# Fewer, wider products of zeros at the start, and one block's loads in another order, in a fused state-space scan and ELU feed-forward kernel

## The chip, the cores and the metric

The kernel runs on one core of a Trainium2 chip. The metric is the device time of one execution in microseconds; 338.59 us is the median of three runs before the change. The engines are TensorE (PE in the profile, PEld for its weight loads), VectorE (DVE), ScalarE (ACT), GpSimd (POOL) and SyncE (SP), whose queue issues nearly all DMAs.

## The reference

Two stages, one after the other. The first is a state-space scan over `x` (4 batches, 8 heads, 768 tokens, 32 features) with decays `a` and vectors `B`, `C` of length 16, in chunks of 32 tokens:

```
cum = cumsum(log(clip(a)))                    # within a chunk
y   = (C B^T * exp(cum_i - cum_j), causal) x  # inside the chunk
    + C state * exp(cum)                      # from earlier chunks
state = exp(sum) * state + sum_j B_j x_j exp(cum_end - cum_j)
```

The second takes the 3072 x 256 result as `x` and computes `elu(x @ w_in) @ w_out`, with `w_in` 256 x 2048 and `w_out` 2048 x 256. The weights arrive as 64-bit floats.

## The kernel before, in words

Tokens are worked in 12 blocks of 256, numbered n from 0; a pair of blocks shares buffers. The scan uses chunks of 64 tokens. Its steps for a block are functions with one line each in the profile: `first_low`, `first_cum` (L501, L512, L520: sums of logarithms into PSUM for blocks 0 and 1) and `first_decays` (L531: their exponentials on ScalarE), `turn_b` (L431, L434: B transposed on TensorE, copied by ScalarE), `mask_heads` (L477), `scores` (L582), `weigh` (L591, VectorE), `scaled` (L422, GpSimd), `sums` (L612: TensorE products of x, in two halves of 128 tokens), `states` (L628, L630 on VectorE, masks L635 on GpSimd), `across` (L661) and `inside` (L679), and the copies of the result into `yT` (L694 VectorE, L696 ScalarE).

The weights come in 16 pieces of 256 x 256, 8 of `w_in` and 8 of `w_out`, loaded by `w_load` (L184, 512 KB each as pairs of 32-bit words) and turned into 32-bit floats by integer steps: `w_abs` (L205, ScalarE, magnitude of the high word), `w_low` (L214, the low word), `w_sign` (L224, VectorE), `w_high_a` (L232, VectorE, clamp), `w_high_b` (L239, VectorE, shift and sign) and `w_sum` (L249, GpSimd, the sum). For pieces 1 to 3 the magnitude lies in a PSUM buffer. `l1(n, i)` (L717) multiplies block n by piece i: four products of 128x128 by 128x256 in plain 32-bit floats, which are eight weight loads and eight matmuls in the trace. `elu` (L731, L738 ScalarE, L739 VectorE) follows one or two products later. From block 2's second half on, `l1_words` (L836) and the second product (L990) work with numbers split into words.

The schedule is written by hand: each engine's instructions stand in the order of the calls, and a semaphore wait holds everything behind it on that engine. PSUM tiles of the pool `a` rotate through seven buffers in the order of allocation, so a tile waits for the reader of the one seven before it. DMAs of SP go out in the order of the calls and share 16 DMA engines.

The program opens with `small_idle_products` (L273): products of a tile of zeros on 32x64 parts of TensorE, in no part of the result. `spare` is a semaphore that no instruction waits for; `l1_words` increments it from TensorE's queue after its matmuls for blocks 4 to 8 (L841), each an instruction record of its own without other effect. TensorE's instructions are fetched during the run by DMA, 16 KB at a time (queue q8 of the profile).

Block one's x, and the weights around it, are asked for by these calls:

```
    w_load(2)
    load_bc(1)
    w_load(3)
    load_x(1, 4)
```

where `load_x(1, 4)` issues the first 128 tokens of x, then `w_load(4)`, then the other 128.

## Time and profile before

| | us |
|---|---|
| median of 3 runs | 338.59 (338.40 to 338.88) |
| the profiled execution | 338.8 |
| its span, first to last instruction | 337.1 |
| PE busy | 330.0 |
| DVE, ACT, POOL busy | 286.9, 259.4, 215.3 |
| DMA, share of 16 engines by q1 | 57.3% |

A busy time says how long an engine had work of its own in the span; matmul ends are modelled, so PE is not at its peak when it is busy. In the views that follow times are microseconds from the span's start. In the chain, a row is a start, a length and what the time went to; in the timeline, a row is start, length, engine, line, operation, output<-input, form and count, and in brackets the engine's idle time before it with what ended it.

### The profile page before, as it was taken

The numbers are of one execution on the slowest core, as the hardware profiler recorded it, in microseconds if no ns is written. First come the engines' busy times: TensorE is split into PE (matmuls) and PEld (weight loads), VectorE is DVE, ScalarE is ACT, GpSimd is POOL, SyncE is SP. The second block draws the span as 40 slices with busy tenths as digits, with TensorE's granted clock in tenths as the row PEclk, the third lists the DMA queues.
The fourth block names the chain that finished last, engine by engine and source line by source line (L and its number), as shares of the span: only waits on it lengthen the run. The fifth ranks groups of instructions, "written<-read, shape, count | busy, mean of one in ns | idle before, by whom it ended". The sixth has DMA issues, their size and how long they took to land.

```text
span 337.1 us, 9871 instructions
## 1 busy us (share of the span) xinstructions
PE 330.0 (98%) x3746; PEld 288.2 (86%) x3746; DVE 286.9 (85%) x511; ACT 259.4 (77%) x537; POOL 215.3 (64%) x242
## 2 busy tenths in 40 slices
PE   8899999999999999999999999999999999999995
PEld 6668888888887888888889889889989999999995
DVE  4998998889897889899989899999996978997942
ACT  5788989599858699857898867798867789897501
POOL 6453554648979396988488978488974355776000
PEclk9999999999999999999999999999999999999999
DMA  8879978657588378660769590889240763330001
GB/s 136 223 215 172 293 182 222 136 116 183 174 154 299 133 202 281 190 197 6 282 184 203 159 289 16 281 209 220 83 147 7 280 206 106 97 125 0 31 2 63
DMA packets 82958, 54.81 MB, mean 163 GB/s; under 512 B 59039, under 2 KB 68575, under 8 KB 82911
## 3 DMA queue, kind: packets, MB, share of 16 engines
q1 hardware_dynamic: 80734, 53.98, 57.3%
q8 instruction: 30, 0.49, 0.6%
q10 hardware_dynamic: 2176, 0.20, 0.5%
q14 instruction: 18, 0.14, 0.1%
HBM read 44.53 MB, written 9.63 MB: 161 GB/s over the span
## 4 chain that ended last, share of the span: by engine, by line
PE 92%; SPq 4%; DMA 2%; issue 0%; DVE 0%; DVEq 0%
PE ps_o L990 24%; PE ps_h L836 20%; PE ps_o L894 12%; PE ps_h L717 11%; PE ps_w L836 10%; PE ps_both L990 6%; PE ps_y L679 2%; DMA xr<-in_x_dram 2%; PE ps_g L582 2%; SPq L184 2%; PE ps_y L661 1%; PE ps_st L612 1%; PE ps_high L990 1%; SPq L140 1%; SPq L156 1%
## 5 line engine op out<-in xcount | busy, mean ns | idle before, releaser
L908 POOL TENSOR_TENSOR g_words<-g_words,g_low 128x512 fp32r<-128x512 f32 x62 | 83.4, 1349 | 48.1 <-ACT e L869 16.4
L990 PE MATMUL ps_o<-o_words,g_words 128*128 128x256 f32 x448 | 83.5, 284 | 0.0
L990 PEld LDWEIGHTS ps_o<-o_words,g_words 128*128 128x128 f32 x448 | 72.8, 190 | 6.3 <-POOL g_words L908 1.5
L869 ACT ACTIVATE e<-ps_h 128x512 f32<-128x512 f32 x72 | 43.0, 597 | 36.1 <-DVE ps_h L857 36.1
L876 DVE SCALAR_TENSOR_TENSOR g<-e,ps_h 128x512 f32<-128x512 f32 x72 | 49.3, 685 | 19.8 <-ACT e L870 17.8
L990 PE MATMUL ps_o<-o_low,g_low 128*128 128x256 f32 x224 | 63.3, 283 | 0.0
L932 DVE SCALAR_TENSOR_TENSOR g_low<-g_words,g 128x512 fp32r<-128x512 f32 x72 | 62.7, 876 | 0.2 <-issue 0.2
L857 DVE SCALAR_TENSOR_TENSOR ps_h<-ps_h,e 128x512 f32<-128x512 f32 x72 | 49.8, 692 | 2.7 <-ACT e L849 2.6
L836 PE MATMUL ps_w<-y_both,w_words 128*128 128x512 f32 x144 | 48.6, 419 | 0.0
L870 ACT ACTIVATE e<-e 128x512 f32<-128x512 f32 x72 | 45.5, 632 | 2.3
L836 PE MATMUL ps_h<-y,w_words 128*128 128x512 f32 x144 | 45.6, 397 | 0.3 <-issue 0.2
L717 PE MATMUL ps_h<-yT,w_in 128*128 128x256 f32 x192 | 44.8, 383 | 1.1 <-ACT yT L696 1.0
L894 PE MATMUL ps_o<-w_out,g 128*128 128x256 f32 x192 | 45.5, 380 | 0.0
L849 ACT ACTIVATE e<-ps_w 128x512 f32<-128x512 f32 x72 | 41.9, 583 | 3.7 <-PE ps_w L836 3.7
L836 PE MATMUL ps_h<-y,w 128*128 128x512 f32 x144 | 44.7, 391 | 0.0
L931 ACT ACTIVATE g_words<-g 128x512 fp32r<-128x512 f32 x72 | 43.6, 624 | 0.0
L990 PEld LDWEIGHTS ps_o<-o_low,g_low 128*128 128x128 f32 x224 | 42.6, 190 | 0.0
L717 PEld LDWEIGHTS ps_h<-yT,w_in 128*128 128x128 f32 x192 | 35.6, 190 | 7.0 <-POOL w_in L249 1.6
L894 PEld LDWEIGHTS ps_o<-w_out,g 128*128 128x128 f32 x192 | 36.1, 189 | 5.5
L836 PEld LDWEIGHTS ps_h<-y,w_words 128*128 128x128 f32 x144 | 26.7, 188 | 7.4 <-issue 1.0
L836 PEld LDWEIGHTS ps_h<-y,w 128*128 128x128 f32 x144 | 27.0, 188 | 6.3
L836 PEld LDWEIGHTS ps_w<-y_both,w_words 128*128 128x128 f32 x144 | 23.6, 190 | 1.8
(132 smaller groups left out, 549.6 us busy)
## 6 DMA issues: line engine op xcount, KB each, us to landing
w_words<-w_kept SPq DMA_DIRECT2D x28, 512.0 KB
w<-w_kept SPq DMA_DIRECT2D x28, 256.0 KB
L<-flat SPq DMA_DIRECT2D x20, 256.0 KB
w<-in_moe_w_out_dram SPq DMA_DIRECT2D x8, 512.0 KB
w_kept<-w_words SPq DMA_DIRECT2D x8, 512.0 KB
w<-in_moe_w_in_dram SPq DMA_DIRECT2D x7, 512.0 KB
xr<-in_x_dram SPq DMA_DIRECT2D x24, 128.0 KB
out_dram<-eo SPq DMA_DIRECT2D x18, 128.0 KB
```

The source lines that it names most:

```text
L717: nc.tensor.matmul(out=ps[:, j], lhsT=w_in[i][:, k, j * P:(j + 1) * P], rhs=yT[n // 2][:, k, n % 2].rearrange("p u i -> p (u i)"), start=( ...
L836: nc.tensor.matmul(out=ps, lhsT=lhs[:, k], rhs=rhs[:, k], start=k == 0 and lhs is not w0, stop=k == KC - 1 and lhs is not w1)
L849: nc.scalar.activation(e, both, ACT.Copy, scale=WORD)
L857: nc.vector.scalar_tensor_tensor(out=high, in0=high, scalar=WORD - 1.0, in1=e, op0=ALU.mult, op1=ALU.add)
L869: nc.scalar.activation(e, high, ACT.Relu, scale=-1.0)
L870: nc.scalar.activation(e, e, ACT.Exp, scale=-1.0)
L876: nc.vector.scalar_tensor_tensor(out=g_tile(n, m // 2)[:, m % 2].rearrange("p b i -> p (b i)"), in0=e, scalar=1.0, in1=h, op0=ALU.subtract ...
L894: nc.tensor.matmul(out=o_of[n][:, ts], lhsT=g_of[n // 2, j][:, m % 2, n % 2, ts * P:(ts + 1) * P], rhs=w_out[j][:, m % 2], start=(m == 0 a ...
L908: nc.gpsimd.tensor_tensor(out=out, in0=in0, in1=in1, op=ALU.subtract)
L931: yield nc.scalar.activation(words[:, 0], g, ACT.Copy, scale=NEAR / WORD)
L932: yield nc.vector.scalar_tensor_tensor(out=low, in0=words[:, 0].bitcast(F32), scalar=WORD, in1=g, op0=ALU.mult, op1=ALU.subtract)
L990: nc.tensor.matmul(out=ps, lhsT=lhs, rhs=rhs, start=lhs is both_g and first > 0 or lhs is g1 and first > 1, stop=last and lhs is not g1, s ...
```

## The change

Four edits. The first products of zeros are 19 of four times 88 columns in place of 39 of two times 86. TensorE's queue gets 2 increments of `spare` after each of the four products of ten `l1` calls, from the second to the eleventh of the run of twelve that starts with block 1's first. Block one's x is loaded whole before piece 4. And for piece 3, the fourth, the magnitude (`w_abs(3)`) moves ahead of two of block one's four decays, its clamp ahead of its sign mask, and the transposes of block one's B take their PSUM buffer before it.

```
-    def load_x(n, piece=None):
+    def load_x(n):
...
-            if piece is not None and u == 0:
-                w_load(piece)
...
-    def small_idle_products(count, cols):
+    def small_idle_products(count, times, cols):
...
-                out=banks[k % 4][at:at + Q, 0:2, 0:cols], lhsT=idle[rows, 0:Q],
-                rhs=idle[rows, 0:cols].unsqueeze(1).to_broadcast([32, 2, cols]),
+                out=banks[k % 4][at:at + Q, 0:times, 0:cols], lhsT=idle[rows, 0:Q],
+                rhs=idle[rows, 0:cols].unsqueeze(1).to_broadcast([32, times, cols]),
...
-    small_idle_products(39, 86)
+    small_idle_products(19, 4, 88)
...
-        nc.scalar.copy(out=s["bt"], in_=tb)
+        return lambda: nc.scalar.copy(out=s["bt"], in_=tb)
...
-    def l1(n, i, by_half=False):
+    def l1(n, i, by_half=False, marks=0):
...
+            for _ in range(marks):
+                nc.tensor.sem_inc(spare, 1)
...
-    load_x(1, 4)
+    load_x(1)
+    w_load(4)
...
     elu()
-    first_decays(1, 0, 1, 2, 3)
+    first_decays(1, 0, 1)
     l1(0, 1)
+    b_turned = turn_b(1)
     w_abs(3)
-    turn_b(1)
+    first_decays(1, 2, 3)
+    b_turned()
     w_low(3, nc.scalar)
+    w_high_a(3)
     w_sign(3)
-    w_high_a(3)
     mask_heads(1)
...
-        l1(n, i, by_half=s == 0)
+        l1(n, i, by_half=s == 0, marks=2 * (0 < s < 11))
```

More of the change, by code (lines that the diff above doesn't have):

```diff
@@ L708, in g_tile @@
         return g_of[n // 2, i]
-    def l1(n, i, by_half=False):
+    spare = tc.alloc_semaphore("spare")
+    def l1(n, i, by_half=False, marks=0):
         ps = psum([P, 2, BLK], "ps_h")
@@ L821, in both_of_y @@
                 in1=y[:, k], op0=ALU.mult, op1=ALU.add)
-    spare = tc.alloc_semaphore("spare")
     def l1_words(n, m, ahead=None, ahead_of_join=(), ahead_of_jobs=()):
```

## The prediction

> **What bounds the kernel now.** I read the page first: the engines' busy times, and the chain that ended last by engine.

> ```profile
> PE 330.0 (98%) x3746; PEld 288.2 (86%) x3746; DVE 286.9 (85%) x511; ACT 259.4 (77%) x537; POOL 215.3 (64%) x242
> ...
> q8 instruction: 30, 0.49, 0.6%
> ...
> PE 92%; SPq 4%; DMA 2%; issue 0%; DVE 0%; DVEq 0%
> ```

> TensorE is the bound over the whole span; 6% of the chain is DMA and its queue. So the next view is the chain in order of time.

> ```profile
> 11.83 2.79 SPq L184
> ...
> 15.80 6.89 DMA xr<-in_x_dram
> 22.69 0.04 issue
> 22.74 0.35 PE ps_st L612 x16
> 23.08 1.92 PE ps_h L717 x8
> 25.01 0.42 PE ps_y L661 x24
> 25.43 0.81 PE ps_y L679 x54
> ```

> The second half of block one's x, queued at 15.80 behind piece 4 of the weights, lands at 22.69, and TensorE waits for it. From 26.73 the chain is TensorE to the end. The matmul records show one larger gap after that, 0.25 us at 106.1. So a gain that reaches 26.73 should reach the end, and what the change does is decided before that time. There I read the timeline by engine (start, time, instruction, idle before it):

> ```profile
> 4.20 1.03 PE L501 MATMUL ps_x<-low,ident 128*128 128x256 bf16 x4
> ...
> 21.61 0.34 PE L612 MATMUL ps_st<-xr,sc 64*32 64x64 f32 x16
> 22.74 0.35 PE L612 MATMUL ps_st<-xr,sc 64*32 64x64 f32 x16 [0.78 <-DMA xr<-in_x_dram]
> ```

> ```profile
> 18.11 1.12 DVE L224 TENSOR_SCALAR mag<-w 128x512 uint32<-128x512 uint32 x1
> 19.15 0.69 DVE L232 TENSOR_SCALAR ps_mag<-ps_mag 128x512 f32<-128x512 f32 x1
> ...
> 22.00 0.75 DVE L591 TENSOR_TENSOR M<-ps_g,L 128x256 f32<-128x256 f32 x2
> 23.12 0.23 DVE L628 COPY S_new<-ps_st 128x64 f32<-128x64 f32 x1 [0.37 <-PE ps_st L612]
> ```

> ```profile
> 18.91 0.80 POOL L422 TENSOR_TENSOR sc<-bc,eb 128x256 f32<-128x256 f32 x1
> 21.09 1.32 POOL L249 TENSOR_TENSOR w_in<-mag,w_in 128x512 uint32<-128x512 uint32 x1 [1.39 <-DVE mag L239]
> ```

> To be seen: TensorE loses 0.78 us to x, but VectorE, which takes the sums next, idles only 0.37 us for it. And the weights of piece 3 are ready at 22.41 (21.09 + 1.32), 0.60 us before the product that needs them starts at 23.01.

> **Idle products: +0.07 us.** 39 products are 78 matmul records. They start in groups of eight, 0.287 us apart, which is 172 columns of two cycles at half the later rate (a full group of L717, 256 columns, takes 0.216 us each). Ten groups: the last starts at 3.74 and ends at 4.03; L501 follows at 4.20. After: 19 products of 352 columns make five groups of 0.287 x 352/172 = 0.587 us. With the first group's extra 0.055 us the last starts at 3.51 and ends at 4.09. So L501 moves from 4.20 to 4.27. Behind it lie block 0's scan and, without idle time over 0.1 us from 9.41 on, VectorE's weighings and piece 0's words; I let the 0.07 go through. Ends: -0.1 (if the wider products pack better) to +0.07.

> **x before piece 4: -0.45 us.** The two transfers on SP swap: x's second half is issued at about 15.18, not 15.80, piece 4 at about 15.70. Piece 4 is 512 KB, 2.1 to 2.5 us at the 200 to 250 GB/s of these slices, so x lands at some 20 to 21, before TensorE asks for it at 21.96. The wait of 0.78 us goes. What is late next, step by step:
> - L612's second half ends at 22.3, not 23.08.
> - VectorE is not free before 22.67: L739 at 21.40 waits for ScalarE's exponential, which ends at 21.37; the two weighings start at 22.00 and end at 22.75, with instructions following each other some 0.08 us before the row's end. The state copy therefore starts at 22.67 instead of 23.12: 0.45 us.
> - TensorE's l1 with piece 3 can start when GpSimd's sum is done, 22.41, plus the 0.1 to 0.15 us seen at 18.94 to 19.00 and 16.51 to 16.66: 22.55 instead of 23.01, 0.46 us, and ends 24.5.
> - GpSimd's four masks (23.42 to 24.81 before) end at 24.36; L661 24.50, not 24.94; L679, whose weighings follow the states on VectorE, and the copies into yT move alike; l1(1, 0) starts at 26.28, not 26.73.

> Piece 4 lands later, near 22.3, where x's last packets ended before. ScalarE wants it at 22.42; a delay there is covered by ScalarE's idle 2.1 us before L696 at 25.87. Behind SP's pair nothing changes: the writes of the running sums are issued after both, as before.

> **Piece four's magnitudes: 0.** (w_abs(3), the fourth piece from 0.) On ScalarE the same seven instructions stand in another order; w_abs(3) moves from 18.21 to about 17.70, two decays go behind it, and the copy of turn_b still finds its transposes (18.87) done. The PSUM buffers also swap: w_abs(3) took the buffer that L739 frees at 18.12, now the transposes take it. VectorE's clamp, on PSUM, can then start at 18.4 and end at 19.1, where the sign mask stood from 18.11 to 19.23. That mask takes 0.42 us where GpSimd rests (25.62); at 18.11 it took 1.12 us, beside GpSimd's sum from 17.67 to 18.94, and at 37.59 0.86 us beside a `scaled` from 37.34 to 38.16. So it is held until GpSimd ends. Moved behind the clamp it is issued at 19.0, when GpSimd's `scaled` (18.91) has begun, which alone takes 0.62 us (7.24): held to about 19.4, done at 19.8. The shift-and-xor comes at 20.3, against 20.27. So the order saves the first hold and buys the second. Ends: +0.15, and -0.3 if the mask gets in ahead of `scaled`; even then the states hang on 22.67. [...]

> **Marks: 0.** 20 products fewer are 80 records (a load and a matmul twice each); 2 x 4 x 10 marks put 80 back by the end of the eleventh l1. In l1_words the trace has 216 such marks (L841), mostly 0.151 us apart at the closest, weight loads and matmuls between them or not. An l1 with 8 marks then needs 8 x 0.151 = 1.21 us of TensorE's queue, 16 other records at 6 ns (as in L679, 128 records in 0.81 us) 0.1 us, together 1.3 us, beside 1.73 us of matmuls. Hidden by 0.4 us; without that cover 10 x 1.21 = 12 us. A semaphore wait of 0.05 to 0.15 us or two per l1 still fits.

> **Instruction fetches: 0.** The 30 packets of q8 are 16 KB, 256 records each, and hold one DMA engine for about 1 us: at 7.52, 12.65, 19.20 and 26.95. Transfers that end beside them end in a tail on one engine: piece 0's last packets to 10.27 where most ended by 9.6, x's second half to 22.34 where most ended by 20.5. With 80 records fewer the first comes near 9.5, behind piece 0, the second at some 13.2, the third after 21. That helps x again, which is no longer waited for. Piece 0 earlier changes little: VectorE is busy until 10.94 anyway. Ends: -0.3 and +0.4. From the last marks on, the fetches fall where they did. [...]

> **Sum.** +0.07 - 0.45 = -0.38 us. The profiled execution took 338.8 us, 1.7 of it outside its span of 337.1; 338.8 - 0.38 = 338.4. It lies 0.21 above the median of 338.59, so the forecast is 338.2. With one term at a time at its end this case runs from 337.9 (-0.3) to 338.6 (+0.4). A measurement of this kernel can tell about 0.2% (0.68 us) from no change; 338.2 is 0.12%.

> **Rivals.**
> - Faster: the head moves too. ScalarE waits 0.61 us for piece 2 (14.93) and then is busy without a pause to past 22.4, and its exponential is what holds VectorE at 21.40. If the second fetch goes behind piece 2, whose tail ends at 14.33, ScalarE's row starts up to 0.61 earlier and the mask slips in ahead of `scaled`: -0.45 - 0.3 to -0.45 - 0.61, 337.5 to 337.9. For it: that tail. Against it: the first transposes of block 1 (18.49) hang on block 0's words on VectorE and GpSimd, not on piece 2, and ScalarE would wait for them.
> - Nothing: the weights of piece 3 come 0.3 to 0.45 later than reckoned, as the mask is held longer, and take x's place: 338.5 to 338.7.
> - Slower: the marks become TensorE's bound. It decides from 1.73 us of queue time per l1: with three waits of 0.15 us beside the marks it is 1.21 + 0.1 + 0.45 = 1.76, and every further 0.15 us costs 10 x 0.15 = 1.5 us: 338.2 + 1.5 = 339.7. Against it: l1_words with marks take 0.92 to 0.93 us per group of four as without (270 us on), and only 3 separate waits are recorded from 30 to 40 us.
> - Slower: the clock. The trace's clock records begin at 5.3 us, with the full rate. If wider products had it granted some 3 us later (as long as they themselves last, 1.10 to 4.2), the 3 us of small products from 5.4 to 8.6 could take twice as long; with half of that on the way to piece 0's words it is +1.5 us, 339.7. Against it: array columns and duration are the same.

> **How the numbers follow.** The forecast's case 0.44, nothing 0.08, the head 0.30, the two slower ones and a fetch in a worse place 0.18 together. Faster by over 0.2% is the head's case and a little of the first: 0.32. Slower is 0.18; within 0.2% is the rest, 0.50. The range 337.4 to 339.0 holds the first three cases and the nearer part of the slower ones; its ends leave out some 0.15.

> **What would show it.** Right: L612's second half without a wait for x; the state copy on VectorE near 22.7 directly behind the weighings; l1 with piece 3 near 22.55, released by GpSimd; l1(1, 0) near 26.3; L224 of piece 3 behind `scaled`. Wrong: l1(1, 0) under 25.9 (the head moved), over 26.6 (something took the place of x), or right at 26.3 and the time given back between 28 and 46, where the marks stand, or after.

## The result

| | before | after |
|---|---|---|
| median of 22 runs each, us | 338.74 (338.00 to 339.34) | 340.38 (338.09 to 341.99) |
| the profiled execution, us | 338.8 | 341.44 |
| its span, us | 337.1 | 339.7 |

The ratio is 1.0050, with a 95% interval of 1.0038 to 1.0061: slower by 1.6 us, where 0.4 us less was forecast. Ratios, here and below, are of fast runs alone (one slow run of 343.5 us, of the kernel after without the x order, is left out of its ratio) and differ slightly from the quotient of the medians. The page of the profile after:

```profile
PE 332.8 (98%) x3706; PEld 289.1 (85%) x3706; DVE 286.9 (84%) x511; ACT 259.3 (76%) x537; POOL 215.1 (63%) x242
...
PEclk9899999999999999999999999999999999999999
...
PE 95%; ACT 2%; DVE 1%; issue 1%; POOL 0%; DVEq 0%; POOLq 0%
```

The 6% of DMA and its queue are gone from the chain, as forecast: x is no longer waited for. But 1% of "issue" has come, time in which TensorE waited for nothing that the profile shows, and TensorE is busy 2.8 us longer (332.8, before 330.0) with 40 matmuls less. The chain in order of time has the place:

```profile
11.97 0.56 PE ps_y L677 x37
12.52 1.26 issue
13.78 0.67 PE ps_y L677 x25
14.45 3.31 PE ps_h L717 x8
...
27.57 0.65 PE ps_y L677 x45
28.23 0.23 issue
```

L677 is `inside`, L679 before: the edits move lines, so the same step has a slightly other number in each kernel (L683 in some of the runs below). TensorE stops in the middle of its 64 products for 1.26 us, and again in block 1's for 0.23. Between them the first `l1` takes 3.31 us where the others take 1.9 to 2.0. The TensorE rows of the timeline, which answer to those shown of before:

```profile
1.10 3.79 PE L271 MATMUL ps_idle<-idle 32*64 32x352 f32 x38 [1.10 <-DVE idle L257]
4.82 1.03 PE L499 MATMUL ps_x<-low,ident 128*128 128x256 bf16 x4
...
24.33 0.51 PE L610 MATMUL ps_st<-xr,sc 64*32 64x64 f32 x32
24.99 1.97 PE L717 MATMUL ps_h<-yT,w_in 128*128 128x256 f32 x8 [0.16 <-DVE g L741]
```

Block one's sums (L610) run in one row without the wait for x, and piece 3's `l1` follows at once. VectorE and GpSimd around them:

```profile
20.71 0.70 DVE L230 TENSOR_SCALAR ps_mag<-ps_mag 128x512 f32<-128x512 f32 x1 [0.41 <-ACT ps_mag L203]
21.32 0.68 DVE L222 TENSOR_SCALAR mag<-w 128x512 uint32<-128x512 uint32 x1
...
24.76 0.75 DVE L589 TENSOR_TENSOR M<-ps_g,L 128x256 f32<-128x256 f32 x2
25.42 0.21 DVE L626 COPY S_new<-ps_st 128x64 f32<-128x64 f32 x1
```

```profile
21.09 0.62 POOL L420 TENSOR_TENSOR sc<-bc,eb 128x256 f32<-128x256 f32 x1
23.26 1.32 POOL L247 TENSOR_TENSOR w_in<-mag,w_in 128x512 uint32<-128x512 uint32 x1 [1.55 <-DVE mag L237]
```

The state copy stands directly behind the weighings, as forecast, but 2.3 us later than before instead of 0.45 earlier. What has moved them all lies ahead.

The windows of TensorE's clock (start to end, length, then busy us and count of PE, PEld, DVE, ACT and POOL, the granted clock, DMA share, GB/s):

```profile
5.00:13.80 8.80, 7.40 (x185) 5.34 (x183) 6.41 (x21) 5.13 (x16) 3.16 (x9) 1.00 1.02 243
13.80:17.20 3.40, 3.40 (x34) 2.61 (x35) 1.92 (x5) 2.57 (x6) 1.00 (x3) 0.50 0.77 184
```

From 13.80 to 17.22 only half the clock is granted, so that `l1(0, 0)` runs at 0.427 us per matmul, not 0.216.

Where the time comes in, by the starts of the `l1` products (us):

| | l1(0,0) | l1(0,1) | l1(0,2) | l1(0,3) | l1(1,0) | end |
|---|---|---|---|---|---|---|
| before | 12.69 | 16.66 | 19.14 | 23.01 | 26.73 | 337.09 |
| after | 14.38 | 19.40 | 21.88 | 24.99 | 29.12 | 339.69 |
| later by | 1.69 | 2.74 | 2.74 | 1.98 | 2.39 | 2.60 |

Of the 2.60 us, 2.39 are there by 29 us. The step from 2.74 to 1.98 is before's wait for x (0.78), which after does not have; the 0.4 that follow are the second stop.

**What stops TensorE.** Number TensorE's recorded instructions (weight loads, matmuls, semaphore instructions) in order of start; these are the records, and a stretch of 256 of them that comes with one packet is a block of instructions here (not one of the 12 blocks of tokens). The first stop lies exactly ahead of record 449, the second ahead of record 961. 449 is 193 + 256 and 961 is 193 + 3 x 256. A packet of q8, 16 KB, seems to hold 256 records: before and after have 7805 each, from 193 on that is 29.7 times 256, and each has 30 packets. For the first blocks the trace gives the time at which TensorE enters a block, the next q8 packet, and the time at which the block after it is entered:

| | block entered | packet | wait for the packet | next block entered | after the packet's end | stop |
|---|---|---|---|---|---|---|
| before, record 193 | 5.54 | 7.52-8.45 | 1.98 | 10.63 | 2.18 | none |
| before, 449 | 10.63 | 12.65-13.81 | 2.02 | 16.59 | 2.78 | none |
| before, 705 | 16.59 | 19.20-20.12 | 2.62 | 25.40 | 5.28 | none |
| after, 193 | 7.68 | 11.19-12.29 | 3.51 | 13.78 | 1.49 | 1.47 |
| after, 449 | 13.78 | 17.87-18.82 | 4.09 | 23.90 | 5.09 | none |
| after, 705 | 23.90 | 26.04-27.05 | 2.14 | 28.46 | 1.40 | 0.45 |

(The stop is counted from the start of one record to the start of the next, so it is up to 0.2 longer than the idle time.) I read this so: when TensorE's sequencer (PEq in the profile's words) enters a block it asks for the next one, which can be used some 1.4 us after its packet has ended (1.49 and 1.40 at the two stops). With a wait for the packet of 2 to 4.1 us and about 1 us of transfer that makes some 4.3 to 6.5 us per block. TensorE takes 256 records in 5.1 us between 5.54 and 10.63 before, and would have taken them in 4.6 from 7.68 after. The 80 records that the change takes out stood in the first block, which the 3.8 us of idle products stretched. With them gone, the start of the next block falls 80 records further on, past the slow starting steps and into the scan.

### The profile page after: what moved, and what is told of

The parts are those of the page before. It is cut to its first block, busy times and chain, and to the rows that moved or that the text cites. A ratio compares the mean times of both kernels' runs of the same rounds, so it can differ in the third digit from the quotient of the medians.

```text
span 339.7 us, 9871 instructions
## 1 busy us (share of the span) xinstructions
PE 332.8 (98%) x3706; PEld 289.1 (85%) x3706; DVE 286.9 (84%) x511; ACT 259.3 (76%) x537; POOL 215.1 (63%) x242
## 4 chain that ended last, share of the span: by engine, by line
PE 95%; ACT 2%; DVE 1%; issue 1%; POOL 0%; DVEq 0%; POOLq 0%
PE ps_o L991 23%; PE ps_h L837 19%; PE ps_h L717 12%; PE ps_o L895 12%; PE ps_w L837 10%; PE ps_both L991 6%; PE ps_y L677 3%; PE ps_g L580 2%; PE ps_y L659 2%; PE ps_st L610 1%; PE ps_high L991 1%; PE ps_idle L271 1%; POOL g_words L909 0%; PE ps_x L510 0%; PE ps_x L499 0%
## 5 line engine op out<-in xcount | busy, mean ns | idle before, releaser
L717 PE MATMUL ps_h<-yT,w_in 128*128 128x256 f32 x192 | 45.8, 390 | 0.2 <-DVE g L741 0.2
L717 PEld LDWEIGHTS ps_h<-yT,w_in 128*128 128x128 f32 x192 | 36.8, 195 | 5.8 <-issue 0.5
L837 PEld LDWEIGHTS ps_h<-y,w_words 128*128 128x128 f32 x144 | 26.6, 188 | 7.3 <-PE ps_w L837 1.0
```

The costliest lines, as they stand in the source:

```text
L717: nc.tensor.matmul(out=ps[:, j], lhsT=w_in[i][:, k, j * P:(j + 1) * P], rhs=yT[n // 2][:, k, n % 2].rearrange("p u i -> p (u i)"), start=( ...
L837: nc.tensor.matmul(out=ps, lhsT=lhs[:, k], rhs=rhs[:, k], start=k == 0 and lhs is not w0, stop=k == KC - 1 and lhs is not w1)
```

## The experiments

The profile of after alone does not say which of the edits does it, nor that it is the number of records. Each result is set against runs of before on the same chip; there were three chips, with medians of before of 338.74, 338.59 and 338.82, so results against different medians come from different chips.

**x alone, whole before piece 4**

```
-    load_x(1, 4)
+    load_x(1)
+    w_load(4)
```

> The kernel before with one edit: block one's x loaded whole before piece 4. All theories that put the loss on the first products (their record count, their length or the clock) expect the gain of my sum, 0.3 to 0.5 us (ratio 0.9985 to 0.999), the sums' wait of 0.78 us gone and l1(1, 0) near 26.3. A theory that puts the loss on the loads expects it slower by over 0.5 us.

Measured: 338.33 against 338.74, ratio 0.9984 (0.9963 to 1.0005). VectorE and TensorE in the timeline:

```profile
22.65 0.21 DVE L628 COPY S_new<-ps_st 128x64 f32<-128x64 f32 x1
```

```profile
22.41 1.99 PE L717 MATMUL ps_h<-yT,w_in 128*128 128x256 f32 x8 [0.40 <-DVE M L591]
```

The state copy stands at 22.65, forecast 22.67; `l1` with piece 3 at 22.41, forecast 22.55, held by VectorE's weighing. The time is 0.41 lower, -0.45 in the prediction, but the interval just holds no change, and the two places don't show what the order is worth: the run with the increments alone, further down, has the old order of x and stands as early.

**Both orders, 39 products**

```
-    load_x(1, 4)
+    load_x(1)
+    w_load(4)
...
-    first_decays(1, 0, 1, 2, 3)
+    first_decays(1, 0, 1)
     l1(0, 1)
+    b_turned = turn_b(1)
     w_abs(3)
-    turn_b(1)
+    first_decays(1, 2, 3)
+    b_turned()
     w_low(3, nc.scalar)
+    w_high_a(3)
     w_sign(3)
-    w_high_a(3)
```

> The kernel before with both orders new (x before piece 4; the magnitude, clamp and PSUM buffer of piece 3), and the 39 small products kept. If the orders are harmless: 0.3 to 0.6 us faster, the clamp before the sign mask costing nothing. If the order of the magnitudes costs what its hold behind GpSimd's scaled suggests, up to 0.15 us less gain than with x alone.

Measured: 338.87 against 338.74, ratio 1.0003 (0.9988 to 1.0018). VectorE:

```profile
18.76 0.70 DVE L232 TENSOR_SCALAR ps_mag<-ps_mag 128x512 f32<-128x512 f32 x1 [0.79 <-ACT ps_mag L205]
19.37 0.42 DVE L224 TENSOR_SCALAR mag<-w 128x512 uint32<-128x512 uint32 x1
...
22.96 0.21 DVE L628 COPY S_new<-ps_st 128x64 f32<-128x64 f32 x1
```

The clamp now waits 0.79 us for ScalarE's magnitude, which itself waits 0.28 for piece 3's DMA and starts at 18.08. The mask is not held here (0.42), yet the state copy comes 0.31 later than with x alone. In this profile that is 0.31 of the 0.47 us between before and x alone there (23.12 to 22.65). The gain that was expected (0.3 to 0.6 us, or up to 0.15 less) is not there, and the median is 0.54 above that with x alone; the two intervals overlap.

**19 wide products alone: 80 records fewer and no increments**

```
-    small_idle_products(39, 86)
+    small_idle_products(19, 4, 88)
```

> The kernel before with the 19 wide products in place of 39, no marks, the old orders. Theory of the code blocks: 80 records fewer put a boundary of TensorE's code in the dense products of block 0, whose block arrives late; a stall of 1 to 1.5 us in L679 near 12.5, the kernel 1.5 to 3 us slower. Theory of the tail: three products over make a last group of their own, L501 at 4.8 in place of 4.2, 0.6 to 1 us slower and no stall inside L679. Theory of the loads: no loss here.

Measured: 344.08 against 338.74, ratio 1.0159 (1.0125 to 1.0193). TensorE, at block 1's scan and at a later one:

```profile
28.03 0.34 PE L683 MATMUL ps_y<-M,xr 64*32 64x64 f32 x15 [1.11 <-issue]
...
103.98 0.96 PE L683 MATMUL ps_y<-M,xr 64*32 64x64 f32 x71 [0.61 <-issue]
```

The loss is larger than expected (1.5 to 3 us), because there are stops beyond the two of the head. The stops lie ahead of records 449, 961, 2753, 4033, 5313 and 6593: all of them 193 plus a multiple of 256, and the last four 1280 apart, five blocks, so that the same place of a scan falls on a boundary time after time. This is what the increments prevent from 50 us on: they bring the later boundaries back to where before has them. They stand behind the two scans at 12 and 27 us, though, and can't help there.

**19 wide products and 20 tiny ones right behind: the records back at once**

```
-    small_idle_products(39, 86)
+    small_idle_products(19, 4, 88)
+    small_idle_products(20, 2, 2, 19)
```

The fourth argument is the number from which k goes on. Both orders are the change's, and there are no increments.

> The changed kernel's wide products and orders, but 20 further products of 4 columns right behind the 19, so that TensorE's queue has 39 products as before; no marks. Theory of the code blocks: no stall in L679 of either block, the first fetch back near 7.5, and only the tail's 0.6 to 1 us lost, less x's 0.4: within 0.6 us of before. Theory of the tail or of the clock by the products' shape: as slow as the change, about 1.6 us.

Measured: 339.13 against 338.74, ratio 1.0023 (1.0004 to 1.0043). The tiny products, of four columns, delay the head, but both stops of the head are gone:

```profile
5.30 0.82 PE L506 MATMUL ps_x<-low,ident 128*128 128x256 bf16 x4
...
13.32 2.33 PE L722 MATMUL ps_h<-yT,w_in 128*128 128x256 f32 x8 [0.80 <-POOL w_in L249]
...
26.78 5.45 PE L722 MATMUL ps_h<-yT,w_in 128*128 128x256 f32 x24
```

Before had `l1(1, 0)` at 26.73, after at 29.12: with the same wide products and the records in their old number the 2.4 us are not there. The 0.2% that are left are not explained.

**19 wide products and the increments, old orders**

```
-    small_idle_products(39, 86)
+    small_idle_products(19, 4, 88)
...
-        l1(n, i, by_half=s == 0)
+        l1(n, i, by_half=s == 0, marks=2 * (0 < s < 11))
```

> The changed kernel without its two new orders: 19 wide products and the 80 marks. Code blocks: boundaries every 256 records, at record 449 of the trace, so the stall in block 0's L679 stays (0.9 to 1.5 us) and one in block 1's (1 us), and none after the marks; some 2 to 2.6 us slower than before. If the marks themselves cost (0.151 us each in TensorE's queue), the stretch of l1 from block 1 on is longer than the 10.6 us per 48 matmuls of before.

Measured: 339.26 against 338.59, ratio 1.0028 (1.0008 to 1.0047). A stop of 1.79 ahead of record 449, none at 961, and half the clock from 15.14 to 18.56. So the stop needs neither order. But the loss is 0.67 us where 2 to 2.6 were expected, and less than half of after's 1.64 (1.71 in after again below, on another chip). The intervals of the ratios overlap a little; how much the two orders add once the stops are there is not settled.

**After with 16 products of four times 107, and 12 increments more**

```
-    small_idle_products(19, 4, 88)
+    small_idle_products(16, 4, 107)
...
-        l1(n, i, by_half=s == 0, marks=2 * (0 < s < 11))
+        l1(n, i, by_half=s == 0, marks=2 * (0 < s < 11) + 3 * (s == 11))
```

> The changed kernel with 16 products of 428 columns in place of 19 of 352 (92 records fewer than before, 92 marks). Tail: four groups of 0.71 us, L501 back at 4.2. If the tail makes the loss, it ends within 0.3 us of before or faster; if the code blocks do, the stall near 12 in L679 stays, about as long, and the kernel is still slower by over 1 us.

Measured: 339.54 against 338.59, ratio 1.0029 (1.0010 to 1.0048). L499 is back at 4.20, and the stops stay: 1.13 ahead of record 449, 0.67 ahead of 961, and 0.37 ahead of 3009. So the later start of the head is not what makes the stops.

**39 products of 214 columns: the later start alone**

```
-    small_idle_products(39, 86)
+    small_idle_products(39, 107)
```

> The kernel before with its 39 products widened from 172 to 214 columns, nothing else: ten groups of 0.36 us, L501 at about 4.9, no record more or less. This is the tail alone. Tail theory: 0.6 to 1 us slower. Code blocks: no stall, and only what the head cannot absorb, 0.3 to 0.6 us.

Measured: 338.74 against 338.59, ratio 1.0005 (0.9993 to 1.0018). L501 starts at 4.91, 0.71 later, and `l1(0, 0)` at 12.80, `l1(1, 0)` at 26.33. The head absorbs it: `l1(0, 0)` waits 0.80 us for the weights of piece 0 all the same.

**x first, 32 products of 214 columns, 30 records put back late in `l1_words`**

```
-    small_idle_products(39, 86)
+    small_idle_products(32, 107)
...
-                    for _ in range(1 + (n > 4 and k == 0)):
+                    for _ in range(1 + (n > 4 and k == 0) + (n == 4 and m < 5)):
...
-    load_x(1, 4)
+    load_x(1)
+    w_load(4)
```

> A version meant to be faster: x before piece 4, 32 products of 214 columns (eight groups of 0.36 us, L501 at 4.2, 28 records fewer), and 30 records put back as marks after the boundary at 106. Code blocks: the request at record 193 comes 28 records later and is still in time for 449; the block that was late at 106.3 is needed about 1 us later, so its stall of 0.4 us goes. 0.4 to 0.8 us faster than before. If 28 records are too many: a stall of some tenths in block 0.

Measured: 338.44 against 338.59, ratio 0.9997 (0.9984 to 1.0009). With 28 records fewer no block boundary stops TensorE, also not at record 3009, where before has a stop of 0.64 us (0.25 of it idle) at 106.30. It was expected to be 0.4 to 0.8 us faster than before; it can't be told from it.

**After again, after without the x order, after without the magnitude order**

The second takes back this edit, in the kernel after:

```
-    load_x(1)
-    w_load(4)
+    load_x(1, 4)
```

The third takes back this one:

```
-    first_decays(1, 0, 1)
+    first_decays(1, 0, 1, 2, 3)
     l1(0, 1)
-    b_turned = turn_b(1)
     w_abs(3)
-    first_decays(1, 2, 3)
-    b_turned()
+    turn_b(1)
     w_low(3, nc.scalar)
-    w_high_a(3)
     w_sign(3)
+    w_high_a(3)
```

> The changed kernel as it is, on one chip with the two that follow. Code blocks: stalls at records 449 and 961, 1.3 to 1.8 us slower than before; the mean granted clock of its runs falls in two groups, about 1.000 and 0.994, the second about 1 us longer.

> The changed kernel with the old order of x and piece 4. If x's 0.4 us carries over, 0.4 us slower than the changed kernel; if the late code has taken x's place (TensorE reaches block 1's sums over 1 us later, when x has landed anyway), the same within 0.2 us.

> The changed kernel with the old order of piece 3's magnitudes. If that order is harmless, the same within 0.2 us; if it is what sets the changed kernel behind the run without both orders (0.3% slower than before, the change 0.5%), 0.5 to 1 us faster than the changed kernel.

Measured, against 338.82: after 340.53 (ratio 1.0048, 1.0031 to 1.0064), without x 339.83 (1.0018, 0.9995 to 1.0042), without the magnitudes 340.14 (1.0045, 1.0026 to 1.0064). Each has both stops, but their lengths differ from profile to profile: ahead of record 449 after again has 0.64, after had 1.47. Four of the 12 runs of after have a mean clock of 0.995 or less and take 341.4 on the mean, the others 340.0. Without the x order TensorE does not wait for x either:

```profile
23.15 0.50 PE L612 MATMUL ps_st<-xr,sc 64*32 64x64 f32 x32
```

By then x has landed. So inside the changed kernel the x order brings nothing that the trace shows. That taking it out makes the median 0.7 us lower, and taking out the magnitudes 0.4, is not settled: the intervals overlap.

**The increments alone: 80 records more from block 1 on**

```
-        l1(n, i, by_half=s == 0)
+        l1(n, i, by_half=s == 0, marks=2 * (0 < s < 11))
```

> The kernel before with the 80 marks alone, so 80 records more from the eleventh l1 on. Code blocks: block 0 and 1 as before, without a stall; the boundaries inside the later scans move 80 records ahead, the block asked for early in a scan is needed 256 records later at its end, and stalls of 1 us or more show at the scans near 101, 158, 208 and 259: 3 to 7 us slower. If only the marks' own queue time counts, no change over 0.2%.

Measured: 345.79 against 338.82, ratio 1.0202 (1.0177 to 1.0226). TensorE at the scan near 100 us:

```profile
99.97 1.29 PE L679 MATMUL ps_y<-M,xr 64*32 64x64 f32 x105
104.15 0.65 PE L679 MATMUL ps_y<-M,xr 64*32 64x64 f32 x23 [2.89 <-issue]
```

Where they stand the increments cost nothing (`l1(1, 0)` at 26.06, and in after the 48 products from 29.12 on take 10.55 us, before 10.63). Far behind, at 104, 214 and 266 us, the boundaries that they have moved stop TensorE for 3.11, 1.37 and 1.55 us. Here the records are too many, in the kernel with the wide products alone they are too few. The first loses 7.0 us, 5.6 of it in the profiled span, with stops of 6.0 in sum; the second 5.3, 4.9 in the span, with 5.9. So it is the number of records ahead that sets where TensorE stops here, whether they are products or increments.

This run also bears on x. Its head has the instructions and the loads of before, and its increments come behind the head, but TensorE does not wait for x:

```profile
21.48 0.48 PE L612 MATMUL ps_st<-xr,sc 64*32 64x64 f32 x32
22.34 1.99 PE L719 MATMUL ps_h<-yT,w_in 128*128 128x256 f32 x8 [0.38 <-DVE M L591]
```

Its `l1(1, 0)` at 26.06 is as early as that with x alone (26.13). With 39 long products, again in the old order, the wait is 0.28 us. So the 0.78 us were those of one execution, and what the order of x is worth on the whole no run here settles.

## Why the prediction was wrong

- **Instruction fetches, 0: the step that failed.** The prediction reckoned the first fetch near 9.5, the second at 13.2, and asked only what their packets do to transfers beside them. That the fetches cost TensorE nothing, the term's 0, no run shows. In the profile of after the packets came at 11.19 and 17.87, and what counted was that TensorE stood ahead of record 449 until 13.78, 1.49 us after the first of them had ended. The view was at hand: the gap at 106.1 that the prediction passed over is such a stop, in the timeline of before:

```profile
105.66 0.40 PE L836 MATMUL ps_h<-y,w_words 128*128 128x512 f32 x1
106.30 0.51 PE L836 MATMUL ps_h<-y,w_words 128*128 128x512 f32 x1 [0.25 <-issue]
```

  It lies between two equal matmuls, ahead of record 3009, 1.39 us after the end of a packet. Most blocks are entered without a stop: of 407 boundaries in the 14 profiles 27 have one of over 0.3 us. Measured price: 1.26 and 0.23 us of TensorE's time in the profile of after, 0.43 and 0.42 in that of after again.
- **x, -0.45: not shown.** The run with x alone fits (-0.41, and both places to 0.15 us), but its interval holds no change, and the wait of 0.78 that the term was read from is 0.28 and nothing in two other profiles with the old order and the head on time. In the sum it is wrong in any case: with block 1's sums 0.7 to 2.7 us late, as in the four profiles of after and its variants, nothing is left to gain. The terms were added as if none changed another's cover.
- **Idle products, +0.07: mis-sized, harmless by themselves.** The first group starts at 1.10, L499 at 4.82, 0.62 later than before. There are six groups 0.587 apart, not five: starts of the matmul records at 1.10, 1.74, 2.33, 2.92, 3.50 and 4.09, the last two with three matmuls each. 19 products, two matmul records each, are two times eight and three: groups of 8, 8, 8, 8, 3 and 3 records, and from 3.50 to 4.09 the first group of three takes as long as one of eight. Of the prediction's two cycles a column the trace of before shows the ratio: from one matmul of 256 columns to the next 0.216 us in f32 (L717), 0.109 in bf16 (L501, from 14.85). That a head 0.7 us later does no harm by itself was shown with 39 long products.
- **Magnitudes, 0, with ends of -0.3 and +0.15.** The picture was wrong (the clamp waits for ScalarE and the DMA of piece 3, not for the mask), except that the mask beside `scaled` is held (0.68 us in after, from 21.32, against 0.42); +0.3 in one profile with the 39 products, nothing that can be told inside the changed kernel.
- **Marks, 0.** Right for their own cost in TensorE's queue (10.55 us for the 48 matmuls, before 10.63); what their records move further on, the prediction did not ask.
- **The rivals.** None had the mechanism; "a fetch in a worse place" shares a chance with the two slower ones, but as something done to transfers. The one on the clock came nearest in time (339.7), but for another reason: the first grant did come later (6.98, before 5.30), which stretches L510 by 0.37 us in the head (1.06, before 0.69). The half clock at 13.80 follows the stop, as the last section works out. In 8 of after's 22 runs the mean clock is 0.995 or less, as one half-rate stretch of 3.41 us in 338 makes it; these take 341.2 on the mean, the other 14 take 339.9.

The account: 339.9 less 338.74 is 1.2 us, in the runs without a half-rate stretch; 1.3 us in 8 of 22 runs is another 0.5. Together 1.7, measured 1.64. In the profile of after again, which has no such stretch, `l1(1, 0)` is 0.86 us later than before (27.59) and the end 1.06. That the stops alone make all of the 1.2 is argued, not shown: the kernel with the products and increments but without the two orders has a stop as well, and loses 0.67.

What stays open: why the packet starts 2 us after a block is entered in one place and 4 in another. The DMA engines are nearly full in one such place (share 0.98 from 6.98 to 10.39 in after, while the weights come in, but 0.77 from 13.81 to 17.22), so the fetch may stand behind the weights' transfers. But in the kernel with 39 long products a block entered at 5.83 had its packet at 6.01, where before one entered at 5.54 had it at 7.52, beside the same weights. No run changed the transfers alone. Open too is what the two orders add to the loss inside the changed kernel.

## What to carry to other kernels

The number of instruction records ahead of a place is part of a hand-made schedule: taking out 80 records that do nothing moved every later block boundary here, and those that fell into a stretch of many small products, due 4.6 us or less after the boundary before them, stopped TensorE (1.26 and 0.23 us in the profile of after). Count the records on the engine's queue, see which instructions the boundaries (here 193 plus multiples of 256) fall on before and after an edit, and put padding back ahead of the first dense stretch, not behind it: 20 tiny products ahead took both stops away, 80 increments behind, in after, left both. And a wait that the profile of before shows is worth its length only if other executions have it too, and if the rest of the edit leaves the engine there on time: take a second profile of before, or look for the wait in runs that leave that place alone.

## What the runs showed of the hardware

The 14 profiles have 407 block boundaries and 27 stops of over 0.3 us at them, from the start of one record to the start of the next. In every one of these TensorE went on 1.27 to 1.60 us after the end of the 16 KB packet. Boundaries that it passed 1.73 us after the end or later have no gap over 0.25. Later a packet sometimes starts before the matmuls at the start of the block have run (in before at 82.61, the block at 84.31; at 283.09, the block at 286.22), so it seems that the sequencer asks when it gets there itself, ahead of the array.

```profile
6.98:10.39 3.41, 3.27 (x90) 2.28 (x74) 1.74 (x6) 2.52 (x9) 1.41 (x3) 1.00 0.98 285
10.39:13.80 3.41, 2.15 (x80) 1.45 (x75) 3.28 (x14) 1.51 (x5) 1.50 (x5) 1.00 0.96 243
```

TensorE was busy for 2.15 of 3.41 us, and the next window had half the clock. So it went behind windows with 1.78 us (the wide products with increments) and 0.75 us:

```profile
100.51:103.92 3.41, 0.75 (x71) 0.58 (x59) 1.29 (x3) 1.46 (x4) 3.41 (x3) 1.00 0.98 363
```

This last is the kernel with the increments alone. Until TensorE's work ends, every window with more kept the clock in the 14 profiles: with 2.25 and 2.46 us in the kernel with the increments alone, and before's with 2.79 us from 12.13. So the limit, if busy time alone sets it, lies between 2.15 and 2.25 us of 3.41 here. After without the x order had a stop of 1.48, as long as after's 1.47, but the beat cut it in two windows of 2.71 and 2.64 busy, and the clock stayed. That would explain why the same kernel loses the clock in some runs only; where the beat falls was not set by any run. In after 1.26 us without TensorE's work within one window was enough.
